# Wk and Wq turned on their way in from DRAM, one transposing DMA each, in a linear-attention plus Mish kernel with a new order of steps

## The chip, the cores and the metric

The kernel runs on one NeuronCore of a Trainium2 chip. The metric is the device time of one execution in microseconds, taken as the median over runs. A core has five engines that run side by side and wait for each other by semaphores: TensorE (PE in the profile, its weight loads PEld), VectorE (DVE), ScalarE (ACT), GpSimd (POOL) and SyncE (SP). DMAs are issued here from SP's and ACT's queues; a queue works in order, so an instruction that waits holds up those behind it.

## What is computed

A LayerNorm, then two branches that are added to the input: a linear attention with 16 heads of 28, whose features are the softmaxes of +pq and -pq, and a Mish MLP. S = 2048, D = 448, F = 1792, all in bf16.

```python
xn = _layernorm(x)                                    # x: 1 x 2048 x 448
q, k, v = split(xn @ wqkv)                            # 16 heads of 28
pq = einsum("bhsd,hdf->bhsf", q, w_phi); pk = the same with k
phi_q = concat([softmax(pq), softmax(-pq)]);  phi_k = the same with pk
kv = einsum("bhsf,bhsd->bhfd", phi_k, v);     z = sum over s of phi_k
o = (phi_q @ kv) / (phi_q . z + 1e-6)
h = xn @ w1 + b1;  act = h * tanh(softplus(h))
return x + o @ wo + act @ w2
```

## The kernel before

The 2048 tokens are 16 tiles of 128 rows (tile t), worked in pairs u = t // 2. For each pair LayerNorm gives xn (a ring of 4 buffers, pair u in buffer u % 4), and xnT, its transpose, feeds every product. The transpose goes one of two ways: on TensorE with an evacuation (steps xt3a, xt1d: pair and evacuating engine), or as a transposing DMA on SP's queue (xt2m and so on, L521).

phi is folded into the weights first. Wpq = Wq x phi and Wpk = Wk x phi are made once, in four row blocks c of 128. Since TensorE takes its left operand turned, Wq and Wk are needed transposed. WqT comes from DRAM in four transposing DMAs (L285), one for each group of four heads (112 rows used of each 128); a copy on DVE repeats its last 64 columns (L289, step qd). Wk comes in plainly (step lkms) and is turned on TensorE: w_tr makes four 128x112 transposes for one row block c (L556), and ACT or DVE evacuates them (steps wtk2a to wtk3d). Then w_mm multiplies block c with Wbd, a block-diagonal phi that POOL makes from the loaded phi and a mask (L544, step bd), four matmuls without overlap (L571), evacuated by ACT (steps wmk0a to wmk3a, wmq0a to wmq3a).

After that, for each pair, TensorE makes q, k and v. Each is 14 matmuls of 448 columns with half the rows of the array, two running at a time, cut in part 1 (8 matmuls) and part 2 (6) on one pair of the eight PSUM banks: step k31 is part 1 of k for pair 3. All of them have line L438, as have the first products of the MLP (f0.11 and so on, 512 columns). ACT takes exp(+k) and exp(-k) (L600), exp(+q) and exp(-q) (L661), and Mish (L680); v is evacuated by ACT or DVE. DVE and POOL normalise phi_k (L608 to L612). TensorE then sums kv over all pairs (L629), divides out per tile (nd, L703 and DVE behind it), and makes the output products: G and wo (L843), g14 and g15 (L805). The last tile's output goes out in two DMAs (L858).

The order is written out by hand as a list of some 300 step names, ORDER. run_order calls the steps in that order; each puts its instructions at the end of its engines' queues, and Program works out which semaphores each has to wait for. take1 and take2 give out the PSUM bank, or the pair of banks, that was used longest ago, so the order settles the bank reuse too. Nothing moves at run time: each engine works its list from the top.

Names used below: lx1, lx2, lx4, lx6 load tiles 2 and 3, 4 and 5, 8 to 11, 12 to 15; lx3 tiles 6 and 7; lx0 tiles 0 and 1 (suffix s: SP's queue, a: ACT's). st is a tile's mean and variance (bn_stats and bn_aggr on DVE; its form for ACT, st4a, is three activations), rs a pair's 1/sigma (p: POOL, a: ACT), xn a pair's normalising. z12 is 12 matmuls on constants ahead of all data (L376). pp0 to pp2, pi, pm, pk, pw, pv are memsets and masks on POOL. e3 is the transposing DMA of tile 3's exp(q) (L669).

Of the kernel before, what the change touches and what calls it, by code (L numbers as in the profile page):

```python
# [148 lines left out]
xt3a wtk3d lqT1 wmk0a wmk1a st2d wmk3a st5d v31d rs1p lqT0 st4d xn1d rs2p lqT3 b1 qd lx6s v32a k31 lx0s wmq1a lx4s pp1
wmq0a xn2p l1ts xt1d st14d st15d wmq2a wmq3a k32 k11 st12d rs7p st9d q11 xt2m st8d k12 st10d xn7d q31 rs4p v11d pp0 q12  # L150
xn4p st11d v12d q21 rs5p st13d q32 q22 xn5p k21 st0d l1m2s l1m0s rs6p xt7m v21d k22 st1d v22a ep e3 rs0p v71a pk xt4m
k71 v72a kn3.1 xn6d k72 xt5m k41 xn0d kn3.0 e2 xt6m xt0m v41d e5 k42 l1m1s v42d e4 q41 v51d q42 e6 e8 v52a kn2.0 k61
# [16 lines left out]
def _kernel(es, nc, A_x, A_wqkv, A_w_phi, A_wo, B_w1, B_b1, B_w2, out):  # L169
# [113 lines left out]

    def load_qT(g, eng):
        dma(eng, lambda e: e.dma_start_transpose(WqT[:, g, 0:D], A_wqkv[:, g * GP:g * GP + P]), w=[("WqT", g)],  # L285
            tag=f"ldWqT{g}")

    def double_qT():
        op("DVE", lambda e: e.tensor_copy(WqT[:, :, D:4 * P], WqT[:, :, D - 64:D]), r=[("WqT", g) for g in range(G)],  # L289
           w=[("WqTd",)], tag="qd")  # L290
# [37 lines left out]
    def p_mask():  # L328
        op("POOL", lambda e: e.memset(mask[:], 1.0), w=[("mask",)], tag="pm0")
# [658 lines left out]
```

## Time and profile before

| | us |
|---|---|
| median of 3 runs (150.27 to 150.96) | 150.6 |
| the profiled execution | 150.35 |
| its span, first to last instruction | 148.3 |
| PE busy | 143.7 |
| DVE busy | 100.7 |
| ACT busy | 72.0 |
| POOL busy | 44.4 |

The profiled execution is 2.05 us longer than its span, which lies around the first and the last instruction. Times inside it count from the span's start. PE's share is 97%, but that is a mean: the first microseconds, in which data and weights arrive, look different from the rest.

### The profile page before, as it was taken

To read this page: it belongs to the slowest core of one execution; us is meant where nothing else is said; L and a number is where in the kernel's file an instruction comes from. 1 tells how busy PE (TensorE), PEld (TensorE's weight loads), DVE (VectorE), ACT (ScalarE), POOL (GpSimd) and SP (SyncE) were. 2 spreads that over 40 slices of the span, in tenths; PEclk is the share of its full clock that TensorE was granted. 3 is DMA by queue.
4 is the path that set the end of the run, shared out by engine and by line. 5 is a ranking of instruction groups with operands and counts; after the bars stand their busy time and mean duration, and the time that the engine had idled before them with its cause. 6 is when DMAs were issued, how large, how long until landed. Compare 5 with 4: busy or idle time off the path is not lost.

```text
span 148.3 us, 3988 instructions
## 1 busy us (share of the span) xinstructions
PE 143.7 (97%) x1731; PEld 75.9 (51%) x1731; DVE 100.7 (68%) x225; ACT 72.0 (49%) x83; POOL 44.4 (30%) x65
## 2 busy tenths in 40 slices
PE   7799999999999999999999999999999999999993
PEld 2456456556555475444454445555555555554452
DVE  0888889897999803003998278896789859983042
ACT  3589889978996899578566653202000000000000
POOL 5428489899899990000000000000000000000000
PEclk9999999999999999999999999999999999999999
DMA  5999998999939989960003300031003300306513
GB/s 123 301 190 346 182 275 130 163 205 256 139 67 174 242 242 267 210 113 0 0 4 62 62 4 0 21 73 34 4 2 66 62 0 4 62 4 186 186 52 134
DMA packets 39997, 17.24 MB, mean 116 GB/s; under 512 B 33964, under 2 KB 39212, under 8 KB 39980
## 3 DMA queue, kind: packets, MB, share of 16 engines
q1 hardware_dynamic: 38800, 16.29, 52.5%
q10 hardware_dynamic: 1180, 0.70, 1.9%
q8 instruction: 13, 0.21, 0.6%
q14 instruction: 4, 0.03, 0.1%
HBM read 7.02 MB, written 1.84 MB: 60 GB/s over the span
## 4 chain that ended last, share of the span: by engine, by line
PE 89%; DMA 6%; DVE 2%; issue 0%; ACT 0%; SPq 0%
PE PS L438 47%; PE PS L843 31%; PE PS L805 3%; DMA Wkv<-in_A_wqkv_dram 3%; DMA xnT<-xn 3%; PE PS L703 2%; PE PS L629 2%; PE PS L571 1%; PE PS L821 1%; DVE stats L467 1%; PE PS L556 1%; PE PS L509 1%; DVE xnT L516 0%; ACT Eq L514 0%; DVE x_all L770 0%
## 5 line engine op out<-in xcount | busy, mean ns | idle before, releaser
L438 PE MATMUL PS<-xnT,W 64*128 64x512 bf16 x392 | 44.8, 376 | 0.0
L680 ACT ACTIVATE actT<-PS,b1T 128x1024 bf16<-128x1024 f32 x28 | 30.1, 1112 | 24.3 <-PE PS L438 24.3
L843 PE MATMUL PS<-W,actT 64*128 64x448 bf16 x392 | 39.3, 349 | 0.0
L438 PEld LDWEIGHTS PS<-xnT,W 64*128 64x128 bf16 x392 | 18.8, 94 | 20.8 <-ACT actT L680 0.5
L843 PEld LDWEIGHTS PS<-W,actT 64*128 64x128 bf16 x392 | 18.1, 94 | 18.1 <-issue 0.3
L612 POOL TENSOR_TENSOR actT<-actT,rSk 128x896 bf16<-128x896 bf16 x16 | 26.6, 1702 | 0.7 <-DVE rSk L610 0.6
L770 DVE TENSOR_TENSOR x_all<-PS,x_all 128x448 bf16<-128x448 f32 (+1 forms) x16 | 9.2, 616 | 11.3 <-PE PS L821 5.6
L718 DVE COPY Sq<-PS 128x16 f32<-128x16 f32 x32 | 4.1, 169 | 18.6 <-PE PS L703 18.5
L608 DVE TENSOR_REDUCE Sk<-actT 128x32 f32<-128x896 bf16 x16 | 16.7, 1043 | 0.0
L600 ACT ACTIVATE actT<-PS 128x896 bf16<-128x896 f32 x16 | 13.8, 950 | 1.0 <-PE PS L438 0.9
L438 PE MATMUL PS<-Wkv,xnT 64*128 64x448 bf16 x112 | 13.2, 349 | 0.0
L438 PE MATMUL PS<-Wpq,xnT 64*128 64x448 bf16 x112 | 12.5, 349 | 0.4 <-DMA xnT<-xn 0.4
L467 DVE BATCH_NORM_STATS2 stats<-x_all 128x6 f32<-128x448 bf16 x16 | 9.7, 608 | 4.1 <-DMA x_all<-in_A_x_dram 4.1
L438 PE MATMUL PS<-Wpk,xnT 64*128 64x448 bf16 x112 | 12.5, 349 | 0.0
L726 DVE TENSOR_TENSOR v_all<-v_all 128x464 f32<-128x464 f32 x16 | 10.3, 642 | 0.6
L722 DVE TENSOR_TENSOR v_all<-PS,Sq 128x464 f32<-128x464 f32 x16 | 10.3, 642 | 0.5
L729 DVE TENSOR_TENSOR xn<-v_all,rden 128x448 bf16<-128x448 f32 x16 | 10.0, 625 | 0.6
L724 DVE TENSOR_TENSOR v_all<-PS,Sq 128x464 f32<-128x464 f32 x16 | 10.1, 631 | 0.0
L661 ACT ACTIVATE actT<-PS 128x896 bf16<-128x896 f32 x10 | 8.6, 921 | 1.1 <-PE PS L438 1.1
L438 PEld LDWEIGHTS PS<-Wpq,xnT 64*128 64x128 bf16 x112 | 5.9, 94 | 5.4 <-issue 0.8
L438 PEld LDWEIGHTS PS<-Wpk,xnT 64*128 64x128 bf16 x112 | 6.0, 94 | 4.4
L438 PEld LDWEIGHTS PS<-Wkv,xnT 64*128 64x128 bf16 x112 | 6.0, 94 | 4.3
(82 smaller groups left out, 126.4 us busy)
## 6 DMA issues: line engine op xcount, KB each, us to landing
W<-in_B_w_dram SPq DMA_DIRECT2D x1, 1568.0 KB, 10.1
out_dram<-x_all SPq DMA_DIRECT2D x7, 224.0 KB, 2.1
W<-in_B_w_dram SPq DMA_DIRECT2D x3, 448.0 KB, 4.1
x_all<-in_A_x_dram SPq DMA_DIRECT2D x2, 448.0 KB, 4.9
x_all<-in_A_x_dram SPq DMA_DIRECT2D x3, 224.0 KB, 3.8
Wo<-in_A_wo_dram SPq DMA_DIRECT2D x2, 336.0 KB, 4.1
...
```

The lines of the kernel that those rows point to most:

```text
L438: ins = e.matmul(o, lhs(c, k), rhs(c, k), start=part == "1" and c == 0, stop=part == "2" and c == 2)
L467: op("DVE", lambda e: e.bn_stats(stats[:, t, :], x_all[:, t, :]), r=[("x", t)], w=[("st", t)], tag=f"bn{t}")
L600: op("ACT", lambda e, s=s: e.activation(E_of(u)[:, s, :, :], two(b, D), ACT.Exp, scale=1.0 if s == 0 else -1.0), r=[pb(b), pb(b + 1)], w=[ ...
L608: op("DVE", lambda e: e.tensor_reduce(Sk[u][:, s, :], Eh(), AX.X, ALU.add), r=[("E", u, s)], w=[("Sk", u, s)], tag=f"Sk{u}.{s}")
L612: op("POOL", lambda e: e.tensor_tensor(Eh(), Eh(), ap_on(rSk[u][:, s, 0:1], [[1, 2 * H], [0, DH]]), ALU.mult), r=[("E", u, s), ("rSk", u, ...
L680: op("ACT", lambda e: e.activation(actT[:, fc, q * 1024:(q + 1) * 1024], bank(b, 2), ACT.Mish, bias=b1T[:, fc:fc + 1]), r=[("b1T",), pb(b) ...
L722: op("DVE", lambda e: e.tensor_tensor(tv(t1[i]), num(0), sx(1), ALU.mult), r=[pb(b), pb(b + 1), ("Sq", i, 1)], w=[("t1", i)], tag=f"ta{t}")
L724: op("DVE", lambda e: e.tensor_tensor(tv(t2), num(1), sx(0), ALU.mult), r=[pb(b), pb(b + 1), ("Sq", i, 0)], w=[("t2",)], tag=f"tb{t}")
L726: op("DVE", lambda e: e.tensor_tensor(t1[i], t1[i], t2, ALU.add), r=[("t1", i), ("t2",)], w=[("t1", i)], tag=f"tc{t}")
L729: op("DVE", lambda e: e.tensor_tensor(o_sb[(t // 2) % 2][:, t % 2, :].rearrange("p (h d) -> p h d", d=DH), t1[i][:, :, 0:DH], ap_on(rden[i ...
L770: op("DVE", lambda e: e.tensor_tensor(x_all[:, t, 0:n], bank(b)[:, 0:n], x_all[:, t, 0:n], ALU.add), r=[pb(b), ("x", t)], w=[("out", t)], ...
L843: ins = e.matmul(bank(places[par][0])[:, 0:D], l, r, start=fresh[par], stop=places[par][2] and i >= len(todo) - 2)
```

## The change

Wk now comes turned from DRAM like Wq, and each of the two in one transposing DMA (load_T, L285 of the new file) that takes 512 columns of wqkv: four blocks of 128 columns, the last of which has 64 that are not its own. The plain load of Wk, its sixteen TensorE transposes, the four evacuations and the memset of Wbd go. Since blocks of 128 cut through heads of 28, the mask and Wbd change: block w meets HEADS[w] heads from head HEAD0[w] on, the four products of a row block overlap in their columns and add up in PSUM, and the rows of phi past 448 are zero (a memset on DVE). Each of Wq's and Wk's last 64 columns is repeated by a copy, one on ACT (qda), one on DVE (kdd). Wv has a tensor of its own, its two tails, those of W1, the load of phi and that of tiles 6 and 7 are split in two steps each, and the outputs' transposes get WkT as a home in Wkv's place. ORDER is new from end to end.

```diff
+HEAD0 = (0, 4, 9, 13)
+HEADS = (5, 6, 5, 3)
+NH = 6
...
-lpa pp2 lx3s pm z12 st6d pi lkms table st7d pw lx1a lkts lba lvma bd rs3t wtk2a xn3d lx2s lqT2 wtk0d st3d pv wtk1a wmk2a
+lp0a pp2 z16 lx1s pi pk st3d pp1 lqT lkT table lx2a pp0 pm lp1a st2d lba bd st4a rs1p st5d lx4a qda rs2a b1 xn1d wmq3a
+xn2d lt6s lx0s wmq1a kdd wmq2a wmq0a xt1b xt2d wmk3a ly0s st6d lt7s st7d st9d wmk2a lvms wmk0a ly1s wmk1a q11 lx6s rs3a
...
-    mask = sb("mask", [GP, 4], FP32)
-    Wraw = sb("Wraw", [GP, G, DH], BF16)
-    Wbd = sb("Wbd", [GP, G, 2, 64], BF16)
+    mask = sb("mask", [P, 4, NH], FP32)
+    Wraw = sb("Wraw", [P, 4, DH], BF16)
+    Wbd = sb("Wbd", [P, 4, NH * DH], BF16)
...
-    WqT = sb("WqT", [P, G, 4 * P], BF16)
+    WqT, WkT = sb("WqT", [P, 4, 4 * P], BF16), sb("WkT", [P, 4, 4 * P], BF16)
...
-    def load_qT(g, eng):
-        dma(eng, lambda e: e.dma_start_transpose(WqT[:, g, 0:D], A_wqkv[:, g * GP:g * GP + P]), w=[("WqT", g)],
-            tag=f"ldWqT{g}")
...
+    def load_T(which):
+        dst, at = (WkT, D) if which else (WqT, 0)
+        dma("SP", lambda e: e.dma_start_transpose(dst[:, :, 0:D], A_wqkv[:, at:at + 4 * P]), w=[("WT", which)],
+            tag="ldWkT" if which else "ldWqT")
+
+    def double_T(which, eng):
+        WT = WkT if which else WqT
+        evac(eng, lambda: WT[:, :, D:4 * P], lambda: WT[:, :, D - 64:D], [("WT", which)], [("WTd", which)], f"qd{which}")
...
-    def w_tr(c, eng):
-        b = take1()
-        to = bank16(b)[0:GP, 0:G * P].rearrange("p (g n) -> p g n", g=G)
-
-        def tr(e):
-            for g in range(G):
-                ins = e.transpose(to[:, g, :], Wk[:, c, g * GP:(g + 1) * GP], ident[:])
-            return ins
-        pe(tr, rows_of("Wk")[:1 if c < 3 else 3] + [("ident",)], [pb(b)], f"wtr{c}")
-        evac(eng, lambda: WT[c // 2][:, c % 2], lambda: to, [pb(b)], [("WT", c)], f"wtre{c}")
+        for n, (w, step, k, heads) in enumerate(((0, 2, 2, 5), (1, 1, 1, 6), (3, 1, 1, 3))):
+            op("POOL", lambda e, w=w, step=step, k=k, heads=heads: e.tensor_tensor(
+                ap_on(Wbd[:, w, 0:1], [[step * NH * DH, k], [DH, heads], [1, DH]]),
+                ap_on(Wraw[:, w, 0:1], [[step * DH, k], [0, heads], [1, DH]]),
+                ap_on(mask[:, w, 0:1], [[step * NH, k], [1, heads], [0, DH]]), ALU.mult),
...
-            for g in range(G):
-                ins = e.matmul(bank(b)[:, g * GP:(g + 1) * GP], lhs(g), Wbd[:, g, :, 0:GP // 2], start=True, stop=True)
+            for w in range(4):
+                n, at = HEADS[w] * DH, HEAD0[w] * DH
+                ins = e.matmul(bank(b)[:, at:at + n], lhs(w), Wbd[:, w, 0:n], start=w == 0, stop=w == 3,
+                               skip_group_check=True)
```

SP's queue at the start of the program, before (W1 is the MLP's first weight, xn2 the normalised pair 2):

```order
L270 DMA x_all<-in_A_x_dram 128x896
L273 DMA Wkv<-in_A_wqkv_dram 128x3x448
L281 DMA Wkv<-in_A_wqkv_dram 64x896 x2
L270 DMA x_all<-in_A_x_dram 128x896
L285 DMA_TRANSPOSE WqT<-in_A_wqkv_dram 128x448 x4
L270 DMA x_all<-in_A_x_dram 128x1792
L270 DMA x_all<-in_A_x_dram 128x896
L270 DMA x_all<-in_A_x_dram 128x1792
L281 DMA W1<-in_B_w1_dram 64x1792 x2
L521 DMA_TRANSPOSE xnT<-xn2 128x7x128 [waits dma_9,dma_10,done_POOL]
```

The same place now:

```order
L269 DMA x_all<-in_A_x_dram 128x896
L285 DMA_TRANSPOSE WqT<-in_A_wqkv_dram 128x4x448
L285 DMA_TRANSPOSE WkT<-in_A_wqkv_dram 128x4x448
L269 DMA x_all<-in_A_x_dram 128x448
L269 DMA x_all<-in_A_x_dram 128x896
L280 DMA Wv<-in_A_wqkv_dram 64x448
L269 DMA x_all<-in_A_x_dram 128x448
L272 DMA Wv<-in_A_wqkv_dram 128x3x448
L280 DMA Wv<-in_A_wqkv_dram 64x448
L269 DMA x_all<-in_A_x_dram 128x1792
L522 DMA_TRANSPOSE xnT<-xn3 128x7x128 [waits dma_4,dma_9,done_DVE]
```

The two big transposes stand second and third, ahead of SP's other loads of x and of Wv; the plain load of Wk and four smaller transposes are gone, and the first transposing DMA of a pair is now pair 3's.

DVE's queue now, from the first result of TensorE that it takes (b1T) to the evacuations of the first two pairs' transposes (xn1 and xn2 are the normalised pairs, WkT<-WkT is the copy kdd, dma_2 the DMA that fills WkT):

```order
L517 CAST b1T<-PS 128x14 [waits done_PE]
L502 TENSOR_SCALAR xn1<-x_all,mv,rstd 128x448 [waits done_POOL]
L502 TENSOR_SCALAR xn1<-x_all,mv,rstd 128x64
L502 TENSOR_SCALAR xn1<-x_all,mv,rstd 128x384
L502 TENSOR_SCALAR xn2<-x_all,mv,rstd 128x448 [waits done_ACT]
L502 TENSOR_SCALAR xn2<-x_all,mv,rstd 128x64
L502 TENSOR_SCALAR xn2<-x_all,mv,rstd 128x384
L517 COPY WkT<-WkT 128x4x64 [waits dma_2]
L517 COPY xnT<-PS 128x512 [waits done_PE]
L517 COPY xnT<-PS 128x896 [waits done_PE]
```

The copy that waits for WkT's DMA stands ahead of both evacuations. Before, the only copy of this kind was that in WqT, behind six bn_stats and two normalised pairs, and DVE waited at this place for TensorE's transposes of Wk.

POOL's queue now, from the memset that ends the step pk to the first 1/sigma (rs1p, the last two rows; actT and Eq0 are the pads pp1 and pp0):

```order
L360 MEMSET KVT 128x512 [waits done_POOL]
L347 MEMSET actT 128x32x8
L347 MEMSET Eq0 128x32x8
L332 MEMSET mask 128x24
L333 AFFINE_SELECT mask<-mask 128x24 [waits done_POOL]
L336 AFFINE_SELECT mask<-mask 128x24 [waits done_POOL]
L547 TENSOR_TENSOR Wbd<-Wraw,mask 128x2x140 [waits dma_59,done_POOL]
L547 TENSOR_TENSOR Wbd<-Wraw,mask 128x168
L547 TENSOR_TENSOR Wbd<-Wraw,mask 128x84 [waits done_DVE,dma_61]
L474 TENSOR_SCALAR lnv<-mv 128x2 [waits done_DVE]
L477 TENSOR_TENSOR rstd<-lnv,mhalf 128x2 [waits done_POOL]
```

The step pk (the mask for kv, with KVT's memset), which came after the last 1/sigma before, now stands ahead of phi's mask, of Wbd and of the first 1/sigma.

More of the change, by code (lines that the diff above doesn't have):

```diff
@@ L21 @@
 G = 4
-GP = 112
 TCW = 512
@@ L147 @@
 ORDER = """
-lpa pp2 lx3s pm z12 st6d pi lkms table st7d pw lx1a lkts lba lvma bd rs3t wtk2a xn3d lx2s lqT2 wtk0d st3d pv wtk1a wmk2a
[L149 to L152, printed above, removed]
@@ new lines @@
+xn3d q21 st8d st14d q12 rs4p xt3m q22 v21d st0d k21 xn4p st15d rs7p l1m2s e3 v11d v22a st11d v12a k22 st10d k11 st12d
+xn7d v31d st13d xt4m st1d k12 k31 l1m0s pv q31 v32d rs0p e2 xt7m rs5a xn0d k32 k41 xn5d q32 e4 v41d k42 rs6p q41 xt0m
+v42d xn6d k71 q42 k72 xt5m l1m1s v71a e6 xt6m kn2.1 v01a k01 lz0a v02d v72d kn1.1 k51 kn4.1 k02 e7 v51a k52 e5 lz1s k61
+kn3.1 v52d kn1.0 k62 l2s q51 q61 q52 kn7.1 q62 f0.11 v61a f1.31 v62a e11 kn5.0 f0.12 kn6.1 f1.21 f1.11 f1.32 e12 e8
+f1.22 kn6.0 kn0.1 f0.21 f1.12 e13 ep f0.22 f1.51 e10 f1.01 f0.121 f1.02 kv6 kv1 kn2.0 kn4.0 f0.122 f1.52 los f0.51 kn3.0
@@ L161 @@
+sto3 wo42 sto5 stt14 sto4 sto6 g15 stt15
 """
@@ L235, in Eq_of @@
         return actT[:, EQ_ROWS[u % 3], :].rearrange("p (i s c) -> p i s c", i=2, s=2)
-    oT_home = [(Wkv, 0, ["Wk", "Wv"]), (Wkv, 14 * P, []), (WqT, 0, ["Wq"]), (Wp[1], 0, ["Wp1"])]
-    home_rows = {"Wk": [("Wk", 0), ("Wt", 0), ("Wt", 1)], "Wv": [("Wv", 0)], "Wq": [("WqT", g) for g in range(G)] + [("WqTd",)],
+    oT_home = [(Wv, ["Wv"]), (WkT, ["Wk"]), (WqT, ["Wq"]), (Wp[1], ["Wp1"])]
+    home_rows = {"Wk": [("WT", 1), ("WTd", 1)], "Wv": [("Wv", 0), ("Wv", 1), ("Wv", 2)], "Wq": [("WT", 0), ("WTd", 0)],
                  "Wp1": [("Wp", 1, c) for c in range(4)]}
@@ L346, in p_pads @@
             op("POOL", lambda e, i=i: e.memset(Eq_of(i).rearrange("p i s (h n) -> p (i s h) n", n=64)[:, :, QP:64], 0.0),
-               w=[("Eqp", i)] + ([("WT", c) for c in range(4)] if i == 0 else []), tag=f"pp{i}")
+               w=[("Eqp", i)], tag=f"pp{i}")
     def p_mask2():
@@ L542, in w_bd @@
     def w_bd():
[L543 to L559 removed]
+        for n, (w, step, k, heads) in enumerate(((0, 2, 2, 5), (1, 1, 1, 6), (3, 1, 1, 3))):
[3 more added lines that the diff above has]
+                ap_on(mask[:, w, 0:1], [[step * NH, k], [1, heads], [0, DH]]), ALU.mult),
+               r=[("Wraw", 0), ("mask",)] if w < 3 else [("Wraw", 1), ("mask",), ("Wraw0",)], w=[("Wbd", n)], tag=f"Wbd{n}")
@@ L561, in w_mm, with lhs @@
     def w_mm(which, c, eng):
         b = take1()
-        def lhs(g):
-            if which:
-                return WT[c // 2][:, c % 2, g, :]
-            return WqT[0:GP, g, c * P:(c + 1) * P]
+        WT = WkT if which else WqT
+        def lhs(w):
+            return WT[:, w, c * P:(c + 1) * P]
         def mm(e):
-            for g in range(G):
-                ins = e.matmul(bank(b)[:, g * GP:(g + 1) * GP], lhs(g), Wbd[:, g, :, 0:GP // 2], start=True, stop=True)
-            return ins
@@ L573, in w_mm @@
-        r = [("WT", c)] if which else [("WqT", g) for g in range(G)] + ([("WqTd",)] if c == 3 else [])
-        pe(mm, r + [("Wbd", 0), ("Wbd", 1)], [pb(b)], f"wmm{which}{c}")
+            for w in range(4):
+                n, at = HEADS[w] * DH, HEAD0[w] * DH
+                ins = e.matmul(bank(b)[:, at:at + n], lhs(w), Wbd[:, w, 0:n], start=w == 0, stop=w == 3,
+                               skip_group_check=True)
+            return ins
+        pe(mm, [("WT", which)] + ([("WTd", which)] if c == 3 else []) + [("Wbd", n) for n in range(3)], [pb(b)], f"wmm{which}{c}")
@@ L734, in oT @@
         i = u % 2
-        home = [("oT", u)] + ([x for n in oT_home[u // 2][2] for x in home_rows[n]] if u // 2 not in homes_taken else [])
+        home = [("oT", u)] + ([x for n in oT_home[u // 2][1] for x in home_rows[n]] if u // 2 not in homes_taken else [])
         homes_taken.add(u // 2)
```

87 lines of the change are left out of this document (38 added, 49 removed).

## The prediction

> **What bounds the kernel now.** First the table of stretches (columns: stretch, its length, then PE, PEld, DVE, ACT, POOL busy with their instructions, granted clock, DMA share, GB/s).
>
> ```profile
> 0.00:18.60 18.60, 16.50 (x153) 8.64 (x153) 12.78 (x39) 13.02 (x23) 9.42 (x29) 1.00 0.93 228
> 18.60:57.00 38.40, 38.36 (x484) 22.75 (x486) 30.98 (x58) 34.38 (x40) 35.02 (x37) 1.00 1.02 195
> 57.00:145.40 88.40, 88.40 (x1086) 44.21 (x1083) 56.18 (x130) 24.55 (x23) 0.00 (x0) 1.00 0.27 60
> ```
>
> From 18.6 us to 145.4 us PE never rests (38.36 of 38.40, then 88.40 of 88.40). So the end is the time at which PE gets going, plus its work, plus what follows its last matmul; only the stretch up to 18.6 us has room. Next the chain that ended last, in order of time (start, length, what; x counts instructions):
>
> ```profile
> 11.56 0.50 PE PS L571 x8
> 12.06 0.41 PE PS L509 x7
> ...
> 14.22 4.29 DMA xnT<-xn
> 18.51 0.14 issue
> 18.64 34.54 PE PS L438 x350
> ```
>
> The chain reaches PE through the transposing DMA of a pair; from 18.64 us PE is the chain. How far was PE by then? The same stretch for L438 alone (PE and PEld behind the length):
>
> ```profile
> 0.00:18.60 18.60, 7.90 (x78) 3.55 (x78) 1.00 0.93 228
> ```
>
> 78 of the 336 matmuls for q, k and v were done. In the new order the first wait for a pair's DMA is at v31 (pair 3), and ahead of it stand q11, q21, q12, q22, v21, k21, v11, v22, v12, k22 and k11: 8+8+6+6+8+8+8+6+6+6+8 = 78 as well. What comes after is the same in kind and number in both kernels (258 more such matmuls, the MLP, kv, nd, the output), so **the sum is the time at which v31 starts, against 18.64 us**. The pace of such matmuls, from a dense place of the timeline:
>
> ```profile
> 32.64 2.83 PE L438 MATMUL PS<-Wpk,xnT 64*128 64x448 bf16 x28
> 35.29 0.75 PE L438 MATMUL PS<-Wkv,xnT 64*128 64x448 bf16 x6
> ```
>
> From start to start 28 take 35.29 - 32.64 = 2.65 us, 0.0946 each, so 78 take 7.38. If PE runs through from q11 on, v31 starts 7.38 us after q11.
>
> **When q11 starts: through POOL, DVE and PE.** What is removed (sixteen transposes, four evacuations) lay in time in which PE waits for data anyway, so I cost it at nothing; what it is replaced by must arrive, below. The row of steps that bounds the head is that behind Wbd:
>
> ```profile
> 1.64 0.09 POOL L321 MEMSET mhalf<- 128x2 f32 x1
> 2.17 0.29 POOL L324 TENSOR_SCALAR_AFFINE_SELECT ident<-ident 128x128 bf16<-128x128 bf16 x1
> 25.77 0.27 POOL L350 MEMSET mask<- 128x56 f32 x1
> 27.41 0.53 POOL L359 MEMSET KVT<- 128x512 uint32 x1
> 1.06 0.10 POOL L329 MEMSET mask<- 112x4 f32 x1
> 12.02 0.31 POOL L346 MEMSET actT<- 128x256 bf16 x1
> 4.00 1.08 POOL L544 TENSOR_TENSOR Wbd<-Wraw,mask 112x224 bf16<-112x224 bf16 x2 [1.06 <-DMA Wraw<-in_A_w_phi_dram]
> 11.00 0.28 POOL L473 TENSOR_SCALAR lnv<-mv 128x2 f32<-128x2 f32 x1 [0.43 <-DVE mv L468]
> 11.36 0.71 POOL L476 TENSOR_TENSOR rstd<-lnv,mhalf 128x2 f32<-128x2 f32 x1
> 12.18 0.16 DVE L489 SCALAR_TENSOR_TENSOR shift<-mv,rstd 128x2 f32<-128x2 f32 x1 [0.27 <-POOL rstd L476]
> ```
>
> In the new order POOL does pp2, pi, pk, pp1, pp0, pm, Wbd, rs1p. The old mask started at 1.06 behind pp2; pi starts there now. From 1.64 to 2.46 it took 0.82: to 1.88. pk, 25.77 to 27.94, takes 2.17: to 4.05. Two pads of 0.31: to 4.67. pm, 1.06 to 1.64, takes 0.58: to 5.25 (24 columns in place of 4 change little, as the 56 of pk show). Wbd: the old two products made 448 columns in 1.08, the new three make 280 + 168 + 84 = 532: 1.28, to 6.53; bounds 1.08, and three at 0.54, 1.62. rs1p takes 0.36 (11.00 to 11.36) and 0.71: to 7.60. DVE hears of it 0.11 later (12.07 to 12.18): 7.71. Then on DVE come xn1, xn2, kdd:
>
> ```profile
> 10.83 0.86 DVE L501 TENSOR_SCALAR xn<-x_all,mv,rstd 128x448 bf16<-128x448 bf16 x3
> 11.68 0.22 DVE L289 COPY WqT<-WqT 128x256 bf16<-128x256 bf16 x1
> 12.49 0.62 DVE L516 COPY xnT<-PS 128x896 bf16<-128x896 bf16 x1
> 0.85 4.65 PE L376 MATMUL PS<-const-bfloat16-1.0 128*128 128x512 bf16 x12 [0.85 <-PEq L973]
> ```
>
> xn1 to 8.57, xn2 to 9.43, kdd to 9.65. PE turns xn2 meanwhile (0.41) and at 9.85 has the sixteen wmk ahead of q11. Eight old ones took 0.50 (chain above), 0.0625 each; the new ones have 133 columns on average for 112. I take 0.07, 1.1 in all; bounds 1.0, and 1.2 by columns. So **q11 starts at 10.95** and v31 at 10.95 + 7.38 = **18.33, 0.31 earlier** than before. The first pair's evacuation (512 of the 896 columns that took 0.62) runs behind kdd and is over by 10.1, hidden behind wmk. If kdd is late, both evacuations, q11, and the statistics behind them on DVE are late with it. The four more matmuls of z16 (4.65 for 12, so until 7.05 for 16) lie where PE waits for WqT; b1 behind them is done before xn1.
>
> **What must arrive in time.** Rows for transposing DMAs: SP's time for an issue in ns (min/median/max); one stretch each of plain loads, of WqT's four, and of the last of these; the time to landing of the last; the first statistics on x.
>
> ```profile
> L285 SPq DMA_TRANSPOSE WqT<-in_A_wqkv_dram x4: 1213/1257/1267, 3.6 to 7.5; - x4
> L738 SPq DMA_TRANSPOSE WqT<-xn x2: 1222/1222/1222, 111.2 to 125.8; - x2
> L669 SPq DMA_TRANSPOSE EqT<-actT x10: 1237/1317/3467, 20.2 to 56.3; - x10
> 3.00:4.00 1.00, 1.00 (x4) 0.39 (x3) 0.36 (x1) 0.00 (x0) 0.01 (x1) 1.00 1.15 324
> 8.00:9.00 1.00, 0.88 (x16) 0.69 (x14) 0.72 (x2) 1.00 (x3) 0.00 (x0) 1.00 1.31 256
> 9.00:10.00 1.00, 1.00 (x12) 0.39 (x9) 0.93 (x3) 1.00 (x3) 0.37 (x2) 1.00 0.69 106
> WqT<-in_A_wqkv_dram SPq DMA_TRANSPOSE x1, 3.1
> 3.64 0.63 DVE L467 BATCH_NORM_STATS2 stats<-x_all 128x6 f32<-128x448 bf16 x1 [3.64 <-DMA x_all<-in_A_x_dram]
> ```
>
> One block of 128x448, seven of 128x128 and eight of them all cost SP 1.21 to 1.24 at the least: an issue does not grow with its blocks. I take 1.3 for four of 128x448; the other end is four times 1.257, 5.0. So WqT is issued at 1.26, WkT at 2.6. One is 448 x 512 x 2 B = 0.459 MB; at 256 GB/s that is 1.8 us. Behind the first x (3.64) and beside the second on ACT's queue, WqT lands at about 6.4, WkT at 8.2. kdd wants WkT at 9.43. WqT is wanted earlier: on ACT its copy (qda, twice DVE's 0.22 at most) and two small steps of rs2a stand behind it, and xn2 wants rs2a at 8.57, so WqT may come until about 7.5. Each has 1.1 us to spare; beyond that, its lateness goes to the end one for one.
>
> [...]
>
> v21 wants Wv: 1.4 MB behind WkT's data at 324 GB/s, so about 12.5, against 10.95 + 28 x 0.0946 = 13.6. v31 wants xnT of pair 3; its statistics (three tiles) and xn3 stand behind the evacuations on DVE:
>
> ```profile
> 9.37 0.59 DVE L467 BATCH_NORM_STATS2 stats<-x_all 128x6 f32<-128x448 bf16 x1
> 10.00 0.18 DVE L468 BATCH_NORM_AGGREGATE mv<-stats 128x2 f32<-128x6 f32 x1
> DMA to landing us min/median/max: 3.0/3.5/4.3
> 13.61 1.76 ACT L600 ACTIVATE actT<-PS 128x896 bf16<-128x896 f32 x2
> 10.84 0.92 ACT L514 ACTIVATE v_all<-PS 128x896 bf16<-128x896 f32 x1 [0.67 <-PE PS L438]
> 146.16 0.33 SPq L858 DMA_DIRECT2D out_dram<-x_all  x1
> ```
>
> Evacuations to 10.7, three times 0.77 to 13.0, xn3 0.86 to 13.9, its DMA lands 3.0 to 4.3 later (third row: all of xnT's): **16.9 to 18.2, just ahead of 18.33**. ACT from q12's end (10.95 + 22 x 0.0946 = 13.0) has three pairs of exp at 1.76 and two v at 0.92 until PE wants the banks for q31: 13.0 + 5.28 + 1.84 = 20.1, against 18.33 + 22 x 0.0946 = 20.4. It holds by 0.3; a later ACT goes to PE one for one.
>
> At the end one store of 224 KB more stands right ahead of the last issue on SP (0.33 at 146.16 before). I take 0.1, as its data can go while the last tile is added; bounds 0 and 1.2 (0.33 and 0.23 MB at 256 GB/s).
>
> **Sum.** 150.35 (the profiled execution: span 148.3, 2.05 around it) - 0.31 + 0.1 = 150.14. It was 0.25 below the median of the runs, so the median to expect is 150.4. About 0.5% (0.75 us) is what a measurement can tell from no change; this is none.
>
> **Rivals.** (a) *A shorter head.* POOL's starts overlap (a pad of 0.31 at 0.81, the next step at 1.06: 0.06 each), and Wbd may take 1.08, wmk 1.0: q11 at 10.3, 149.7, or 149.4 where ACT's own start is early too. Against it: xn2 waits for rs2a behind x and WqT. (b) *The wait for xnT takes the old one's place.* With a landing of 4.3 and DVE, or the x that the DMA also waits for, 0.7 late, v31 starts at 18.9: 151.0. For it: the same wait was the last before; its margin is 0.1 to 1.4. (c) *Slower: issue or flow grow with the blocks*, 5.0 us per DMA. WkT is then issued from 6.3 to 11.3 and lands 1.9 behind its issue (3.1 - 1.26), at 13.2; then kdd and wmk, q11 at 14.6, and the x behind it on SP is late as well, v31 at 22.2: 150.4 + 3.9 = 154.3. It decides from WkT after 9.4 or WqT after 7.5; WkT at 11.3 makes 152.3. For it: at 9 to 10 us the old four flowed at 106 GB/s, no faster than SP issued them. Against it: the three issue rows. That the transposes go and nothing is won by it is the forecast itself.
>
> **Chances.** Forecast 0.50 (own range 149.8 to 151.1), (a) 0.17, (b) 0.15, (c) 0.18, of which half below 152.8. The range 149.3 to 152.8 leaves out some 0.05 below and 0.09 above. Faster (below 149.85): (a) and the forecast's edge, 0.22. Slower (above 151.35): (c) and the edges of (b) and the forecast, 0.24. Within: 0.54.
>
> **What would show it.** In the new profile: two issues of 1.3 us on SP, WkT's wait absent ahead of kdd (c); Wbd over at 6.5; q11 at 10.95 (a); v31 at 18.3 without a wait, or with one for xnT (b); PE full from there on. A PE that idles between 20 and 57 us for ACT would make the forecast wrong from the slow side.

## The result, and the profile after

| | before | after |
|---|---|---|
| median of 6 runs, us | 150.31 (149.76 to 150.96) | 152.04 (151.13 to 152.72) |
| the profiled execution, us | 150.35 | 151.52 |
| its span, us | 148.3 | 149.7 |

The changed kernel is slower: ratio 1.0106, 95% interval 1.0063 to 1.0149. The forecast was no change (150.4). The time lies inside the stated range (149.3 to 152.8), but above the forecast's own (149.8 to 151.1). Here and below a ratio compares undisturbed runs alone, so that a median can lie above what its ratio gives.

First the chain that ended last in the changed kernel, in order of time (start, length, what).

```profile
10.03 0.93 PE PS L563 x16
10.96 10.91 PE PS L439 x114
...
21.92 0.97 issue
22.89 1.62 DVE xn L502 x6
24.52 5.23 DMA xnT<-xn
29.75 0.14 issue
29.88 22.13 PE PS L439 x218
```

The head has become what was forecast: the sixteen wmk, then TensorE runs (the chain counts q11's matmuls from the end of the last wmk, the timeline from their own start). These are the rows of TensorE's timeline for q11, for v31, for the last eight matmuls ahead of the stall and for the first eight behind it:

```profile
10.89 2.82 PE L439 MATMUL PS<-Wpq,xnT 64*128 64x448 bf16 x28
18.27 0.92 PE L439 MATMUL PS<-Wv,xnT 64*128 64x448 bf16 x8
28.13 0.94 PE L439 MATMUL PS<-Wv,xnT 64*128 64x448 bf16 x8
29.88 0.93 PE L439 MATMUL PS<-Wv,xnT 64*128 64x448 bf16 x8 [0.81 <-DMA xnT<-xn]
```

But at 29.88 the chain leaves TensorE once more, for a transposing DMA of a pair (pair 0, the fourth of the six that come by DMA), issued at 24.52 and 5.23 us under way. Next the table of stretches (length, then PE, PEld, DVE, ACT, POOL busy, granted clock, DMA share, GB/s).

```profile
18.27:57.00 38.73, 37.91 (x404) 20.54 (x402) 33.34 (x59) 31.13 (x38) 25.94 (x20) 1.00 1.07 214
57.00:146.20 89.20, 89.20 (x1169) 46.27 (x1166) 56.38 (x130) 27.15 (x26) 3.94 (x5) 1.00 0.25 51
27.00:28.00 1.00, 1.00 (x14) 0.62 (x12) 1.00 (x4) 0.64 (x2) 0.00 (x0) 1.00 2.53 184
28.00:29.00 1.00, 1.00 (x12) 0.40 (x8) 1.00 (x3) 1.00 (x2) 0.00 (x0) 1.00 0.54 6
29.00:30.00 1.00, 0.18 (x4) 0.14 (x4) 0.66 (x2) 1.00 (x2) 0.23 (x1) 1.00 0.49 105
```

From v31 (18.27) on, TensorE is short of work in one place, between 29 and 30 us, and just before it the DMA engines move 6 GB/s, though they count as busy for 0.54 of that microsecond. SP's queue around that place (start, length, instruction):

```profile
19.35 0.58 SPq L276 DMA_DIRECT2D W<-in_B_w_dram  x1
19.97 1.24 SPq L661 DMA_TRANSPOSE EqT<-actT  x1
21.25 1.83 SPq L522 DMA_TRANSPOSE xnT<-xn  x1
23.13 1.34 SPq L661 DMA_TRANSPOSE EqT<-actT  x1
24.52 2.79 SPq L522 DMA_TRANSPOSE xnT<-xn  x2
27.35 0.58 SPq L276 DMA_DIRECT2D W<-in_B_w_dram  x1
```

and the times from issue to landing of all six transposing DMAs of xnT:

```profile
DMA to landing us min/median/max: 2.9/4.7/5.2
```

The median landing was 3.5 before; it is 4.7 now. The plain loads at 19.35 and 27.35 are chunks of W1 (128 x 1792 in bf16, 459 KB each), which stand between the transposes. In the old order two chunks were issued from 15.5 on, while SP waited for xn, and the third at 30.8, behind the last pair's transpose.

The end of the changed kernel, and last the same DVE instruction before:

```profile
144.79 1.87 SPq L853 DMA_DIRECT2D out_dram<-x_all  x3
146.73 0.23 DVE L783 TENSOR_TENSOR x_all<-PS,x_all 128x64 bf16<-128x64 f32 x1
146.99 0.33 SPq L850 DMA_DIRECT2D out_dram<-x_all  x1
```

```profile
145.91 0.23 DVE L791 TENSOR_TENSOR x_all<-PS,x_all 128x64 bf16<-128x64 f32 x1
```

From the last DVE instruction to the end of the span: 149.7 - 146.96 = 2.74 us now, 148.3 - 146.14 = 2.16 before. So the two spans differ by three terms: v31 starts 0.37 earlier (18.27 for 18.64); from there to the last DVE instruction it takes 128.69 for 127.50, 1.19 more; the tail 0.58 more. Together 1.40, as the spans do. Of the 1.19, the stall at 29.88 is 0.99: the eight matmuls ahead of it started at 28.13 and such eight take 0.76 from start to start, so the next, v01, was due at 28.89.

### The profile page after: what moved, and what is told of

Same layout as the page of the kernel before. It is cut to its first block, busy times and chain, and to the rows that moved or that the text cites. A ratio compares the mean times of both kernels' runs of the same rounds, so it can differ in the third digit from the quotient of the medians.

```text
span 149.7 us, 3958 instructions
## 1 busy us (share of the span) xinstructions
PE 144.5 (97%) x1719; PEld 76.0 (51%) x1719; DVE 103.0 (69%) x228; ACT 71.6 (48%) x88; POOL 38.7 (26%) x55
## 4 chain that ended last, share of the span: by engine, by line
PE 86%; DMA 6%; DVE 3%; issue 1%; POOL 1%; ACT 0%; ACTq 0%
PE PS L439 45%; PE PS L835 31%; DMA xnT<-xn 3%; PE PS L797 3%; DMA Wraw<-in_A_w_phi_dram 3%; PE PS L695 2%; PE PS L621 2%; DVE xn L502 2%; PE PS L813 1%; PE PS L563 1%; POOL rstd L477 0%; PE PS L510 0%; DVE x_all L762 0%; ACT L317 0%; ACTq L301 0%
## 5 line engine op out<-in xcount | busy, mean ns | idle before, releaser
L835 PE MATMUL PS<-W,actT 64*128 64x448 bf16 x392 | 38.9, 349 | 0.0
L439 PE MATMUL PS<-Wv,xnT 64*128 64x448 bf16 x112 | 12.8, 349 | 0.8 <-DMA xnT<-xn 0.8
L439 PE MATMUL PS<-Wpk,xnT 64*128 64x448 bf16 x112 | 12.5, 349 | 0.0
L439 PE MATMUL PS<-Wpq,xnT 64*128 64x448 bf16 x112 | 11.8, 349 | 0.0
L468 DVE BATCH_NORM_STATS2 stats<-x_all 128x6 f32<-128x448 bf16 x15 | 9.1, 607 | 3.6 <-DMA x_all<-in_A_x_dram 3.5
L439 PEld LDWEIGHTS PS<-Wv,xnT 64*128 64x128 bf16 x112 | 5.8, 94 | 5.8 <-DVE rSk L602 1.2
L517 DVE CAST v_all<-PS 128x896 bf16<-128x896 f32 x5 | 5.3, 1077 | 4.7 <-PE PS L439 4.7
```

The source lines that it names most:

```text
L439: ins = e.matmul(o, lhs(c, k), rhs(c, k), start=part == "1" and c == 0, stop=part == "2" and c == 2)
L468: op("DVE", lambda e: e.bn_stats(stats[:, t, :], x_all[:, t, :]), r=[("x", t)], w=[("st", t)], tag=f"bn{t}")
L835: ins = e.matmul(bank(places[par][0])[:, 0:D], l, r, start=fresh[par], stop=places[par][2] and i >= len(todo) - 2)
```

## Experiments

Each kernel is the changed one with the edit shown, unless the text says otherwise. The ratio is to the kernel before, run on the same chip. The experiments ran on four chips, so rows are best compared by their ratios.

| | median, us | ratio to before, 95% |
|---|---|---|
| changed kernel | 152.04 | 1.0106 (1.0063 to 1.0149) |
| e1_x0_first | 151.96 | 1.0127 (1.0094 to 1.0161) |
| e2_x_first | 154.64 | 1.0206 (1.0168 to 1.0244) |
| e4_v7_first | 151.38 | 1.0076 (1.0053 to 1.0099) |
| e5_tail | 151.77 | 1.0093 (1.0058 to 1.0128) |
| w1_off | 151.01 | 1.0025 (0.9996 to 1.0054) |
| before_w1_on | 152.51 | 1.0130 (1.0080 to 1.0180) |
| phi_early | 153.62 | 1.0189 (1.0146 to 1.0232) |
| all_four | 152.84 | 1.0144 (1.0101 to 1.0188) |
| three_moves | 151.27 | 1.0056 (1.0037 to 1.0076) |
| three_rs | 150.77 | 1.0047 (1.0024 to 1.0071) |
| split_loads | 157.48 | 1.0480 (1.0457 to 1.0502) |
| wbd_split | 151.03 | 1.0049 (1.0019 to 1.0079) |
| w1_off_tail | 151.02 | 1.0021 (0.9992 to 1.0050) |
| wbd_split_tail | 151.18 | 1.0009 (0.9979 to 1.0039) |

### Is it the place of pair 0's transpose on SP? (e1_x0_first, e2_x_first)

e1:

```diff
-rs5a xn0d k32 k41 xn5d q32 e4 v41d k42 rs6p q41 xt0m
+rs5a xn0d k32 k41 xn5d q32 xt0m e4 v41d k42 rs6p q41
```

> One step moved: the transposing DMA of pair 0 (xt0m) goes ahead of that of tile 4's exp(q) (e4) on SP's queue; nothing else changes. Theory T (SP's order): in the changed kernel xt0m was issued at 24.52, 0.8 us after its data (xn0) was ready, behind e4; now it is issued at about 23.8, lands 5.2 us later at 29.0 and TensorE's 1.0 us stall ahead of v01 shrinks to 0 to 0.2. Part of that comes back at k61, whose pair 6 transpose lands at 34.9 while TensorE would now be there at 34.3: a new stall of about 0.5. Net 0.4 to 0.9 us less than the changed kernel, about 151.4. Rival Q (the DMA queues as a whole pause until 29.6, whatever stands in front): xt0m lands at 29.7 as before, the stall stays 0.8 to 1.0, and the time stays at 152.0. Rival B (the big transposes of Wq and Wk made xn0 itself late): no change either, but then xt0m would still wait for xn0, not for SP.

e2, besides that:

```diff
-st1d k12 k31 l1m0s pv
+st1d k12 k31 pv
-xt5m l1m1s v71a e6 xt6m kn2.1
+xt5m v71a xt6m e6 l1m1s l1m0s kn2.1
```

> As the first one, and also the two W1 chunks (l1m0s, l1m1s) and tile 6's exp(q) transpose (e6) go behind the last pair's transposing DMA (xt6m). Theory T: xt0m is issued at about 23.8 and lands at 29.0 or earlier, xt6m is issued at 28.3 instead of 29.97 and lands at 33.2, ahead of TensorE's need at 34.3; stalls between 28 and 45 us fall from 1.0 to at most 0.2, the time by 0.8 to 1.2 us against the changed kernel, to about 151.0. Rival Q (the queues' pauses set the landings): xt0m still lands near 29.7, stalls of about 1 us remain, 152.0. Rival W (W1 becomes the late one): the first product of the MLP, needed at 38.7, waits for the chunks issued at 33 to 35.

In e1's profile (of its slowest execution, 153.21) the stall at v01 went, and the chain shows a new one at the last pair, whose transpose was issued at 31.17:

```profile
11.47 19.70 PE PS L439 x207
31.17 5.02 DMA xnT<-xn
36.19 0.14 issue
36.32 1.51 PE PS L439 x14
```

That is the stall that theory T foretold for k61, but it is 1.5 us and not 0.5, and the time did not fall. In e2 no transpose of x is late. There TensorE waits 2.7 us at the MLP's first product (TensorE's timeline, then SP's, then the landing of the load issued there at 37.48):

```profile
42.16 1.04 PE L439 MATMUL PS<-xnT,W 64*128 64x512 bf16 x8 [2.68 <-DVE rSk L602]
```

```profile
32.19 1.06 SPq L276 DMA_DIRECT2D W<-in_B_w_dram  x2
33.29 1.24 SPq L661 DMA_TRANSPOSE EqT<-Eq  x1
34.57 2.87 SPq L661 DMA_TRANSPOSE EqT<-actT  x1
37.48 0.59 SPq L280 DMA_DIRECT2D W<-in_B_w_dram  x1
```

```profile
W<-in_B_w_dram SPq DMA_DIRECT2D x1, 224.0 KB, 4.5
```

The view names DVE as the releaser, but by the program that product waits for v52's evacuation on DVE, done by 38.9, and for all of W1. The last tail of W1 landed at 37.48 + 4.5 = 41.98, and the product came at 42.16. That is rival W, only by the tail and not by a chunk; the tail stands behind two transposes, and these behind the two chunks. In e1 too the same product waited 0.4 us (tail landed 41.24, product at 41.41). So an order that shuffles this queue moves the stall to whoever is next in it. Theory T, the place of one DMA, falls as the cause.

### Is it the DMA that TensorE waits for? (e4_v7_first)

```diff
-kn2.1 v01a k01 lz0a v02d v72d kn1.1
+kn2.1 v72d v01a k01 lz0a v02d kn1.1
```

> Only TensorE's order changes: the second part of v for pair 7 (v72d, six matmuls, 0.57 us) goes ahead of v01, the instruction that stalled for pair 0's transposing DMA. No DMA is moved. Theory T: the landing stays at 29.75, TensorE arrives 0.57 us later, so the stall falls from 1.0 to about 0.4; everything behind it comes 0.57 earlier, and at k61 the margin to pair 6's transpose (0.3 in the changed kernel) turns into a stall of about 0.25. Net 0.3 to 0.6 us less, about 151.6. Rival E (the stall is made of evacuation, bank or issue, not of the DMA): the stall stays near 1.0 at v01 and the time at 152.0.

The median is 151.38; theory T gave 0.3 to 0.6 us less, about 151.6. The intervals of the two ratios overlap, so that gain is not resolved. What TensorE waited for between 18 and 50 us (total, times, longest):

```profile
PE PS L439 <- DMA xnT<-xn: 0.8, 2, 0.5
```

In this profile v01 does not wait; pairs 7 and 6 do, behind landings of 5.2 and 5.0 us. All that TensorE waits for here are transposing DMAs of x, no bank and no evacuation: rival E falls.

### The W1 chunks, both ways (w1_off, before_w1_on)

In the changed kernel and in e1, e4 and e5, pair 7's transpose was issued 1.9 us behind a chunk of W1 and took 4.8 to 5.2 us; in e2, where that chunk was gone, 3.0. w1_off takes the two chunks ahead of pairs 7 and 6 away. l1m2s goes into SP's gap ahead of all transposes, l1m1s behind the last of them, and l1m0s takes the place at 15.7 that l1m2s had, 2.2 us ahead of pair 4's transpose, where a chunk stays:

```diff
-q12 rs4p xt3m q22
+q12 rs4p l1m2s xt3m q22
-st15d rs7p l1m2s e3 v11d
+st15d rs7p l1m0s e3 v11d
-st1d k12 k31 l1m0s pv
+st1d k12 k31 pv
-xt5m l1m1s v71a e6 xt6m kn2.1
+xt5m v71a e6 xt6m l1m1s kn2.1
```

> The changed kernel with only the three loads of W1's chunks (459 KB each) moved on SP's queue: l1m2s ahead of pair 3's transposing DMA (into SP's gap at 9.9 to 13.9), l1m0s to where l1m2s was (15.7), l1m1s behind the last pair's transposing DMA (xt6m). Theory V (a chunk that is issued 1 to 3 us ahead of a transposing DMA in the same queue delays its landing by the chunk's own transfer, about 2 us): pair 7's transpose lands in 3.0 to 3.5 us instead of 4.8 to 5.2, pair 0's in 3.3 to 4, pair 6's in 3.5 to 4 instead of 4.1 to 5.0; TensorE's stalls for xnT between 18 and 45 us fall from 0.8 to 1.5 us to at most 0.3; time 0.7 to 1.2 us under the changed kernel's 152.0, that is 150.9 to 151.3. Rival Q (the queue pauses of itself, chunks or not): landings stay spread over 3 to 5 us, and the time stays within 0.3 of 152.0. Rival W (W1 late): a stall at the MLP's first product, needed at about 39.

```profile
18.00:57.00 39.00, 38.99 (x416) 21.24 (x414) 34.34 (x62) 32.20 (x38) 27.48 (x24) 1.00 1.06 208
```

```profile
DMA to landing us min/median/max: 2.9/3.8/4.2
```

In the table of stretches TensorE is busy for 38.99 of 39.00 us, no transpose of x takes more than 4.2, and the time is 151.01. before_w1_on does the opposite to the kernel before:

```diff
-st0d l1m2s l1m0s rs6p xt7m
+st0d l1m2s rs6p xt7m
-pk xt4m k71
+pk l1m0s xt4m k71
-e2 xt6m xt0m v41d e5 k42 l1m1s v42d
+e2 l1m1s xt6m xt0m v41d e5 k42 v42d
```

> The kernel before, with only two loads of W1 moved to places like those they have in the changed one: l1m0s from 15.5 us to directly ahead of pair 4's transposing DMA (xt4m), l1m1s from 30.8 to directly ahead of pair 6's (xt6m). Theory V: pair 4's transpose is issued 0.6 later and lands in about 5 us instead of 3.0, at 27.0, against TensorE's need at 25.8: a stall of 0.6 to 1.2; pair 6's lands at 32.5 to 33 against 31.1 plus that stall: 0.3 to 0.8 more. Time 0.9 to 1.7 us over 150.2, that is 151.1 to 151.9. Rival Q: only the 0.6 us of issue are lost, the margins of 1.3 and 0.8 cover them, and the time stays within 0.3 of 150.2.

Its chain, from the issue of the chunk on, and its one wait of TensorE from 18 to 60 us:

```profile
22.66 0.58 SPq L277
23.29 5.75 DMA xnT<-xn
29.17 27.36 PE PS L438 x274
```

```profile
PE PS L438 <- DMA xnT<-xn: 2.0, 1, 2.0
```

The transpose behind the chunk takes 5.75 us, where the same pair's took 3.0, and TensorE waits 2.0 us. The kernel becomes 1.3% slower with nothing changed but two loads. This profiled execution (153.66) has a second delay, which is not the edit's. In the head TensorE stood from 4.99 to 6.95 for a load of Wkv, and after that the granted clock (the last figure but two) was halved:

```profile
8.00:10.00 2.00, 2.00 (x22) 1.90 (x21) 1.08 (x4) 1.57 (x4) 0.00 (x0) 0.50 1.29 198
```

So TensorE was due at this pair 1.2 us later than in the kernel before (27.00 for 25.83). The four runs whose clock stayed at 1.0 took 152.17 to 152.72, and 1.7 us or more above the 150.46 of the kernel before remain.

Now the landings of three pairs, over all profiles that have the new order (issue to landing, us):

| transposing DMA | a chunk of W1 ahead of pairs 7 and 6 (6 profiles) | those chunks moved (8 profiles) |
|---|---|---|
| pair 7, 1.9 us behind the first chunk | 4.8 to 5.6 | 3.0 to 4.3 |
| pair 6, 1.9 to 3.1 us behind the second | 4.1 to 5.0 | 3.5 to 4.2 |
| pair 0, between the two | 3.3 to 5.2 | 4.2 to 5.3 |

**A transposing DMA issued shortly behind a chunk of W1 on the same queue lands later, by about 1 us for pairs 7 and 6 and by 2.7 for pair 4 in before_w1_on; and where the chunks stand is worth most of what the change lost, some 0.8%** (1.0106 to 1.0025, with intervals that just do not overlap). What this does not explain is the landing of pair 0, the one that TensorE waited for in the changed kernel's profile. It is no shorter without the chunks, as in three_moves:

```profile
xnT<-xn SPq DMA_TRANSPOSE x1, 5.3
```

The chunk ahead of it had landed at 23.45 (19.35 + 4.1), before it was issued. For this DMA rival Q stands. So by which of the waits, at pairs 7, 0 and 6, the 0.8% comes back is not shown; nor was it separated which of the three chunks does how much.

### The tail (e5_tail)

```diff
-g14 G62 sto2 ot4m wo41 wo62 wo7H sto3 wo42 sto5 stt14 sto4 sto6 g15
+g14 G62 wo62 sto2 ot4m sto6 wo41 wo7H sto3 wo42 sto5 stt14 sto4 g15
```

> Only the tail: the second part of pair 6's output product (wo62) goes directly behind G62, and its store (sto6) directly behind the transpose ot4m, so that two stores of 224 KB or less, not three, are issued in the last 3 us. Theory S (the last stores queue for the DMA engines): from SP's last issue (end 147.32) to the end of the span took 2.4 us in the changed kernel against 1.8 in the one before; it falls to about 1.8 to 2.0, and the time by 0.4 to 0.6 us, to about 151.5. Rival N (the last landing does not depend on what is queued ahead of it, 0.57 is scatter): 152.0, unchanged. TensorE's stall at v01 stays, 0.8 to 1.2, in both.

The last DVE instruction ends at 146.27 and the span at 148.8: 2.53 us for 2.74. The edit was clumsy: sto6 now stands on SP's queue ahead of two stores (sto3, sto5) whose data, by the order, is made before its own; how long it held them up was not measured. Theory S gave 0.4 to 0.6 us; 0.2 came, and the ratio hardly moved (1.0093 for 1.0106). In eight profiles with the tail of the changed kernel this stretch was 2.72 to 2.82, and 2.16 and 2.23 in the two with the old tail, so the 0.6 against before is no scatter. This run holds a second reading. Up to the tail it is the changed kernel, and yet its profiled execution (150.59) has no stall. Its pair 0's transpose was issued at 24.28, at the same place of the same order, and landed so:

```profile
xnT<-xn SPq DMA_TRANSPOSE x1, 3.3
```

3.3 us where the other execution took 5.2. With nothing changed ahead of it, the landing of this DMA varies by 2 us between executions; the order decides whether TensorE has the slack to bear it. In the changed kernel's profile pair 0's products were due 4.37 us behind its issue (28.89 - 24.52).

### The turned loads (split_loads)

```diff
-        dma("SP", lambda e: e.dma_start_transpose(dst[:, :, 0:D], A_wqkv[:, at:at + 4 * P]), w=[("WT", which)],
-            tag="ldWkT" if which else "ldWqT")
+        for w in range(4):
+            dma("SP", lambda e, w=w: e.dma_start_transpose(dst[:, w, 0:D], A_wqkv[:, at + w * P:at + (w + 1) * P]),
+                w=[("WT", which, w)], tag=("ldWkT" if which else "ldWqT") + str(w))
```

> The changed kernel with one part undone: Wq and Wk each come in four transposing DMAs of 128 columns, not in one of 512. Theory (the single DMA costs SP's queue 2.0 and 2.5 us, a DMA of 128 columns 1.2 to 1.3 as in the kernel before): the eight take 10 us in place of 4.5, WkT lands at 13 to 14 instead of 9.2, SP's later loads of x and of Wv are issued 5.5 us later, and the head waits for them: 3 to 5 us longer, 155 to 157. Rival B (the single large DMA is what made the changed kernel slower): 0.5 to 1 us shorter than 152.0.

SP's timeline here, and the row of the single DMA's issue in the changed kernel (ns, min/median/max):

```profile
1.25 5.11 SPq L286 DMA_TRANSPOSE WqT<-in_A_wqkv_dram  x4
6.40 5.15 SPq L286 DMA_TRANSPOSE WkT<-in_A_wqkv_dram  x4
```

```profile
L285 SPq DMA_TRANSPOSE WkT<-in_A_wqkv_dram x1: 2487/2487/2487, 3.3 to 3.3; - x1
```

Four small issues cost 5.1 us, one large 2.0 (WqT) or 2.5 (WkT), and the kernel with eight is 5.4 us slower. Part of this is the clock: in the profile TensorE had one matmul to do between 6.97 and 9.84, and behind that the granted clock was 0.50 from 9.5 to 12.5. Rival B falls: without the single DMA the kernel is longer, not shorter.

### The head (phi_early, all_four, three_rs, wbd_split)

In the changed kernel's profile POOL's last product of Wbd waited 0.18 us for the second load of phi. phi_early:

```diff
-lqT lkT table lx2a pp0 pm lp1a st2d
+lqT lkT lp1a table lx2a pp0 pm st2d
```

> The changed kernel with only the second load of phi (lp1a, 3.5 KB) moved one place up on ACT's queue, ahead of the table load and of the load of tiles 4 and 5. Theory H (it lands too late for the last Wbd product: it was seen to land 6.30 to 6.90 us after the start in five profiles of this head, and the chain that ends last ran through it each time): it lands before 5.8, POOL does the last Wbd product at 6.2 without a wait, and everything behind it comes 0.2 us (against the changed kernel's profile) to 0.6 us (against the other profiles) earlier: v31 at 18.0 to 18.1, time 151.5 to 151.8. Rival L (POOL's own list or the load of Wk is next late at once): no change, 152.0.

POOL's and ACT's timelines in phi_early; then the same ACT instruction in the changed kernel; last, from phi_early's chain, SP's issue of WkT's DMA:

```profile
5.10 1.37 POOL L547 TENSOR_TENSOR Wbd<-Wraw,mask 128x280 bf16<-128x280 bf16 x3
```

```profile
6.58 0.58 ACT L460 ACTIVATE junk<-x_all 128x448 bf16<-128x448 bf16 x1 [3.40 <-DMA x_all<-in_A_x_dram]
```

```profile
4.48 0.58 ACT L460 ACTIVATE junk<-x_all 128x448 bf16<-128x448 bf16 x1 [1.88 <-DMA x_all<-in_A_x_dram]
```

```profile
3.83 3.67 SPq L285
```

POOL no longer waits, as theory H said, but the load of tiles 4 and 5, issued 0.58 later, arrives 2.1 us later, and ACT's statistics and the copy of WqT stand behind it: q11 comes at 11.45 for 10.89. The rest came by SP. Its issue of WkT took 3.67 us for 2.49, Wv and the later x came late behind it, and TensorE waited 0.5 us for Wv and 1.6 for transposes of x. The ratio rose by 0.8%, which neither theory gave; why both DMAs took longer was not tested. all_four joined this with three other moves and showed the same ACT wait; in its profile, too, TensorE had little to do (7.0 to 9.5 us) and the clock was halved behind that, until 12.5.

> The changed kernel with four moves together: W1's chunks off the transposes, phi's second load early, v72d ahead of v01, and the tail's store of pair 6 early. If the causes add: 1.0 + 0.3 + 0.2 + 0.2 us less than 152.0, about 150.3, level with the kernel before (150.2); stalls for xnT 0, end of the last DVE step to end of the span 2.5. If the queue pauses of itself, or a new engine becomes the bound (DVE's row of reductions from 33 to 42 us, which was without a gap in one experiment): 151.0 to 151.5.

three_moves leaves phi alone and sets w1_off, e4's move and a tail in another order together:

```diff
-g14 G62 sto2 ot4m wo41 wo62 wo7H sto3 wo42 sto5 stt14 sto4 sto6 g15
+g14 wo7H G62 wo62 ot4m sto2 sto3 sto5 stt14 wo41 wo42 sto6 sto4 g15
```

> The changed kernel with the W1 loads off the transposes (as in w1_off, 151.0), v72d ahead of v01, and the tail in another order: wo7H, G62 and wo62 directly behind g14, and on SP's queue the four stores whose data is ready (sto2, sto3, sto5, stt14) ahead of those of pairs 6 and 4, so that two stores, not three, are issued in the last 3 us ahead of the last tile's. Theory S (the last stores queue for the DMA engines): from the last DVE step to the end of the span 2.2 to 2.4 us instead of 2.74, time 0.3 to 0.5 under w1_off, 150.5 to 150.7. v72d should add nothing where no transpose is late any more. Rival N (the tail does not depend on what is queued): 151.0.

No gain over w1_off in the runs (1.0056 for 1.0025), with a tail of 2.55 in its profile. three_rs adds one move:

```diff
-lba bd st4a rs1p st5d
+lba rs1p bd st4a st5d
```

> As three_moves, and on POOL the 1/sigma of pair 1 (rs1p, 0.9 us) goes ahead of the three products of Wbd. Theory H (the head hangs on the second load of phi, which lands at 6.3 to 6.9, and on what POOL does behind it): xn1 no longer waits for it and is ready at about 8.0 instead of 9.4; Wbd is complete at 7.5 instead of 6.7, Wpq's products end at about 9.5 and the transposes of pairs 1 and 2 follow at once: q11 0.2 to 0.4 us earlier, time 0.2 to 0.4 under three_moves, 150.2. Rival P (TensorE's products of Wpq, now later by 0.8, are what the head waits for): the same time or up to 0.3 longer.

```profile
6.74 1.38 POOL Wbd L547 x3
8.12 0.05 issue
8.16 1.10 PE PS L563 x16
...
146.23 0.19 DVE x_all L783
```

The phi load left the chain and the tail is 2.2 us (148.6 - 146.42), as before the change, with the same order of stores that gave 2.55 in three_moves; but q11 came at 10.90 because Wbd is now late. The median fell by 0.5 to 150.77, but the ratio only from 1.0056 to 1.0047, within both intervals; it is still above the kernel before. wbd_split does two of the three products of Wbd ahead of rs1p and the third behind it.

> As three_rs, but POOL does the first two products of Wbd ahead of rs1p and the third, which waits for the second load of phi, behind it. In three_rs Wbd was complete at 8.12 and TensorE's Wpq products started with it; POOL had idled for 0.8 us ahead of rs1p. Theory H: Wbd is complete at 7.3 to 7.4, q11 comes at 10.3 to 10.6 instead of 10.97, and the time is 0.3 to 0.5 under three_rs: 150.3 to 150.5, level with the kernel before. Rival T (pair 3's transpose, which landed at 17.5 in three_rs against a need at 18.35, is next late): v31 comes no earlier than 17.6, a gain of at most 0.3 if the load lands as late as in other profiles; then 150.5 to 150.8. What neither changes is the 0.3 to 0.4 us that TensorE, without a gap in both, takes longer from v31 to its end than in the kernel before.

q11 came at 10.53 and v31 at 17.92, and the profiled execution, the fastest of twelve, took 150.47. The others lie between 150.55 and 153.05, the median is 151.03, and the ratio (1.0049) is that of three_rs: the 0.4 us won in the head do not show in it.

### The spread that is left (w1_off_tail, wbd_split_tail)

To w1_off and to wbd_split the same edit, since the last tail of W1 had no slack in w1_off:

```diff
-xt6m l1m1s kn2.1 v01a k01 lz0a ... e5 lz1s k61
+xt6m l1m1s lz1s kn2.1 v01a k01 lz0a ... e5 k61
```

> w1_off and one load more: the last tail of W1 (lz1s, 224 KB) goes from behind e7, e5 to directly behind l1m1s on SP's queue. In w1_off it was issued at 34.79 and landed at 38.99, and the MLP's first product, which needs it, started at 39.15: no slack left. Theory V2 (with the chunks off the transposes, the W1 tail at the end of the same queue is what makes runs spread): it is issued at about 31 and lands at 35.5; the median falls by 0.2 to 0.4 under w1_off (151.0), to 150.6 to 150.8, and the slow ones of the runs go. Rival Q2 (the spread comes from the transposes' own landing): 151.0 and the same spread.

> wbd_split with the same load moved (lz1s directly behind l1m1s). wbd_split's runs lay between 150.5 and 152.3 with a median of 151.0; TensorE comes 0.6 us earlier there, so a W1 tail that lands at 38.3 or later (issued at 34.12, landing 3.7 to 4.5) makes it wait. Theory V2: median 150.4 to 150.6, the spread below 1 us. Rival Q2: 151.0, spread as before.

Neither median moved to speak of. The runs lie between 150.63 and 151.69 (w1_off: 150.41 to 151.60), and between 150.3 and 151.4 but for one (wbd_split: 150.47 to 152.34 but for one). What TensorE waited for in the two profiles (11 to 60 us), w1_off_tail first:

```profile
PE PS L439 <- DMA xnT<-xn: 0.2, 1, 0.2
```

```profile
PE PS L439 <- DMA Wv<-in_A_wqkv_dram: 0.6, 1, 0.6
```

With W1's tail out of the way it is pair 3's transpose, behind a load of x that took 5.8 us, or a load of Wv. Theory V2's fall of the median did not come. That the spread left is that of the landings of loads and transposes is likely from these two waits, not shown. wbd_split_tail is level with the kernel before (1.0009, 0.9979 to 1.0039); none of these kernels beats it.

## Why the prediction was wrong

- *Head: right.* q11 was put at 10.95 and came at 10.89; the pace of 0.0946 us gave 7.38 for the 78 matmuls, measured 18.27 - 10.89 = 7.38; v31 at 18.33 forecast, 18.27 measured, without a wait. The steps between agree too (1/sigma at 7.60 and 7.69), so this is no luck. One link was missed and cost little: Wbd's last product waited 0.18 for phi.
- *Arrivals: right where they were checked.* Pair 3's xnT landed at 13.94 + 2.9 = 16.84 (16.9 to 18.2 forecast). ACT held at q31, which started at 20.36, without a wait (20.4 forecast).
- *The issue of a big transpose: wrong by size, harmless.* 1.3 us were taken; it is 2.03 for Wq, 2.49 for Wk. WkT landed at 3.32 + 5.9 = 9.2 and not 8.2, just in time for kdd. Eight blocks of 128x128 had shown no growth (1.24 at the least, against 1.21 for one of 128x448); four of 448x128 from DRAM do. The data came later behind its issue, too: WkT landed 3.4 us after the end of its issue (3.32 + 2.49 = 5.81), not the 1.9 that rival (c) takes.
- ***The step that failed*: "What comes after is the same in kind and number in both kernels", so "the sum is the time at which v31 starts", and "PE full from there on".** The same in kind and number is not the same in order. Of six transposing DMAs only the first, pair 3's, was held against TensorE's need. The other five follow on a queue in which the new order had put chunks of W1 between them. The fourth had 4.37 us from its issue to TensorE's need, took 5.2, and cost 0.99; over the fourteen profiles with the new order it took 3.3 to 5.3. The order of SP's queue was shown up to the first of them and not beyond. What moving the chunks gives back, some 0.8%, is shown by w1_off; that the chunks made this very DMA late is not.
- *Rival (b)*, a wait for xnT in the place of the old one, was the right mechanism at the wrong pair: it was priced for pair 3 alone.
- *The range: luck.* It reached up to 152.8 for rival (c), big DMAs that issue or flow too slowly, and that is not what happened.
- *The tail: mis-sized.* 0.1 taken (bounds 0 and 1.2), 0.58 measured.
- *Not foreseen, and left open:* without any stall TensorE still takes 127.9 us from v31 to the last DVE instruction in w1_off (146.39 - 18.49), 127.50 before. These 0.4 us were not tested. In the chains 0.3 of them lie with the products of q, k, v and the MLP's first (67.3 for 67.0) and 0.1 with the sum over kv, which is cut in two places now (3.39 for 3.27).

The sum, redone with what was measured: 150.35 - 0.37 (head) + 0.99 (stall) + 0.20 (rest of that stretch) + 0.58 (tail) = 151.75, against a profiled 151.52 (the time around the span was 1.82 there and 2.05 before). The median, 0.5 above that, has no profile of its own. The 0.25 that the forecast added for the median came from three runs; six put the median before at 150.31, level with its profiled 150.35.
